# Batched attention with an FFN behind it: score halves and column groups in stretches of sixteen products, and a written order of products from step 48

## The chip, the cores and the metric

The kernel runs on one core of one Trainium2 chip. The metric is the device time of one execution in microseconds. Matrix products run on TensorE (PE), and everything they write lands in PSUM, eight banks of 512 f32 columns on 128 partitions. ScalarE (ACT) and VectorE (DVE) empty those banks, GpSimd (POOL) does elementwise work in SBUF, and SyncE (SP) issues nearly all DMAs.

## What is computed

Eight batches of eight heads, 576 tokens, 64 channels. A first attention packs keys and values into 32 slots a head; a second lets the queries read these slots; a leaky FFN of 2048 columns follows, all in f32.

```python
p_packed = sm_attn(p, k, v)                 # 32 packed slots a head
out = sm_attn(q, p_packed, p_packed)        # B, H, S, D
x = transpose(out).reshape(4608, 512)
h = x @ w_in                                # 512 -> 2048
g = maximum(h, 0) + alpha * minimum(h, 0)
return g @ w_out                            # 2048 -> 512
```

## The kernel before

**Halves and steps.** A batch has two halves of 288 tokens, `k = 2b` and `2b + 1`. The FFN of a half goes through 16 blocks `f` of 128 columns, so a batch takes 32 steps and the program 256, each with one `first(k, f)` and one `second(k, f)`. The kernel never forms x: it multiplies the packed values p' by w_in once a batch (`packed_w`, four column groups `j` of 512 columns, each written as a pair of numbers hi and lo that add up to f32), and `first` multiplies these by the attention weights `a` of the second softmax, also held as a pair: six products of 128x128 weights and 288 columns (L572 to L574, three for each half of the heads) into one bank of the pool `ps_h`, which has two. Then ACT takes relu(-h) (`neg`, L580), DVE adds alpha's part (L581), ACT casts that to `gh` (L591), and DVE takes the rest `gl` (L592). Without the flag `from_sbuf` L581 writes its result back into the bank, which is then held until L592 has read it; with it the result goes into `neg` in SBUF, and the bank is free after L581. `second` (L610 to L612) multiplies gh and gl by w_out: twelve products into the four accumulators of `ps_a`, which are copied out after the last block of a half (L627, L629).

**Attention of the next batch** is cut into pieces that run between the steps: `attention(b)` and `packed_w_steps(b)` are generators that do one piece at each step of a list. With T = 32(b - 1) the pieces of batch b lie at steps T + 3 to T + 20, and its four column groups at T + 21, 25, 29 and 33; the first step that needs them is T + 32. Their banks come from `ps_m`, which has two. Scores are taken in halves `hf` of 288 columns: eight products (L317), one for each head, of 64x32 weights, into two banks, one for each `r` of two head groups. Scores of p and k are copied to SBUF by ACT (L360), those of q and p' are transposed into SBUF by DVE (L450). A column group of p' w_in is also eight products of 64x32 weights, with 512 columns (L516), into two banks; ACT (L535) and DVE (L536) both read each bank. The values are packed by forty products of 128x32 weights in one stretch (L428).

**What sets the order.** The program is written in order of steps, `first` of step i, the pieces of step i, `second` of step i - 2, and a scheduler puts the instructions of each engine in an order of its own, by priority and by its estimate of when operands and buffers are ready. `tc.issue_after(ins)` keeps what follows behind an instruction; before, the pieces of a step stand behind `first` of that step (`marks`) by this, but nothing ties one FFN product to another. Two score halves, or two column groups, are therefore two stretches of products with FFN products between them: there are two banks in `ps_m`, and the first pair has to be emptied first.

```python
gs[k, f] = (gh, gl)
...
order += [(k, f, (0, NF)) for k in range(4, 2 * B) for f in range(NF)]
```

## Time and profile before

| | |
|---|---|
| time, median of three runs | 735.76 us (735.74 to 736.73) |
| span of the profiled execution | 733.9 us |
| PE busy | 715.7 us, 98% of the span |
| PE weight loads busy | 648.9 us |
| DVE, ACT, POOL busy | 421.4, 355.7, 59.7 us |
| granted PE clock | full from slice 5 on |
| FFN products (L610 to L612; L572 to L574) | 2976 of 295 to 299 ns; 1440 of 295 to 299 ns |
| column groups of p' w_in with 512 columns (L516) | 480 records of 601 ns |
| scores into ps_m (L317) | 448 records of 415 ns |

The profile states the span of its execution; the time of a run also holds what lies around the span, and the median of the runs is 1.9 us above it. PE products overlap in the array, so a product's duration is longer than the distance to the next one, and the distance is what counts. A product with f32 operands (scores, p' w_in, transposes, packed values) shows as two records, an FFN product as one. A row with x16 is a merged row: its first start, and the time from there to the end of its last record. Rows of the timeline give the start from the beginning of the span, the duration, and in brackets the idle time before and what ended it.

### The profile page before, as it was taken

How to read it: one execution, taken by the hardware profiler on the slowest of the kernel's cores; microseconds unless marked ns; L12 is line 12 of the kernel's file. 1: busy time of each engine (PE TensorE's matmuls, PEld its weight loads, DVE VectorE, ACT ScalarE, POOL GpSimd, SP SyncE). 2: the span in 40 equal slices, each digit the busy share in tenths (PEclk: the TensorE clock that was granted, in tenths of full speed). 3: DMA queues.
4: the chain of work that ended last, by engine and by line, in shares of the span. 5: the costliest groups of instructions: out<-in, count | busy, mean ns of one | idle time of the engine just before them, and what ended most of it. 6: DMA issues, size and time to landing. Idle time of an engine off the chain costs nothing.

```text
span 733.9 us, 15803 instructions
## 1 busy us (share of the span) xinstructions
PE 715.7 (98%) x6346; PEld 648.9 (88%) x6346; DVE 421.4 (57%) x859; ACT 355.7 (48%) x813; POOL 59.7 (8%) x80
## 2 busy tenths in 40 slices
PE   5799999999999999999999999999999999999997
PEld 3466898999889999899989998989988999989997
DVE  3898988857545464545644465453654446453443
ACT  3686698944434343443444543344444434343332
POOL 1001200004000030001200021000300003000000
PEclk8899999999999999999999999999999999999999
DMA  9996554234324222424223241332231401210000
GB/s 301 375 318 223 203 199 147 68 99 155 126 92 146 81 92 108 145 72 130 90 103 104 93 134 63 117 129 92 97 116 66 147 2 38 82 34 1 31 4 34
DMA packets 51386, 85.45 MB, mean 116 GB/s; under 512 B 4464, under 2 KB 31088, under 8 KB 51312
## 3 DMA queue, kind: packets, MB, share of 16 engines
q1 hardware_dynamic: 51024, 84.14, 33.9%
q8 instruction: 50, 0.82, 0.5%
q10 hardware_dynamic: 288, 0.30, 0.1%
q14 instruction: 24, 0.20, 0.1%
HBM read 70.79 MB, written 13.63 MB: 115 GB/s over the span
## 4 chain that ended last, share of the span: by engine, by line
PE 92%; DVE 3%; ACT 2%; DMA 1%; issue 1%; SPq 1%; ACTq 0%; DVEq 0%
PE acc L612 19%; PE acc L610 18%; PE acc L611 18%; PE ps_h L572 9%; PE ps_h L574 9%; PE ps_h L573 9%; PE ps_m L516 4%; PE ps_m L317 2%; PE ps_m L428 1%; DMA vtwo<-in_v 1%; PE ps_h L569 1%; PE ps_m L411 1%; SPq L170 1%; DVE w L134 0%; DVE w L130 0%
## 5 line engine op out<-in xcount | busy, mean ns | idle before, releaser
L610 PE MATMUL acc<-gh,wo 128*128 128x288 f32 x992 | 283.2, 297 | 0.0
L611 PE MATMUL acc<-gh,wo 128*128 128x288 f32 x992 | 282.5, 295 | 0.0
L612 PE MATMUL acc<-gl,wo 128*128 128x288 f32 x992 | 239.6, 299 | 0.0
L581 DVE SCALAR_TENSOR_TENSOR ps_h<-neg,nal,ps_h 128x288 f32<-128x288 f32 x208 | 107.8, 521 | 170.9 <-ACT neg L580 170.3
L580 ACT ACTIVATE neg<-ps_h 128x288 f32<-128x288 f32 x256 | 105.8, 414 | 206.1 <-PE ps_h L574 200.3
L610 PEld LDWEIGHTS acc<-gh,wo 128*128 128x128 f32 x992 | 186.3, 188 | 4.7 <-issue 3.1
L611 PEld LDWEIGHTS acc<-gh,wo 128*128 128x128 f32 x992 | 186.2, 188 | 2.1 <-issue 1.7
L612 PEld LDWEIGHTS acc<-gl,wo 128*128 128x128 f32 x992 | 166.9, 188 | 22.5 <-issue 22.4
L572 PE MATMUL ps_h<-a_h,pw 128*128 128x288 f32 x480 | 143.6, 299 | 0.0
L574 PE MATMUL ps_h<-a_h,pw 128*128 128x288 f32 x480 | 141.9, 296 | 0.0
L573 PE MATMUL ps_h<-a_l,pw 128*128 128x288 f32 x480 | 141.5, 295 | 0.0
L592 DVE TENSOR_TENSOR gl<-ps_h,gh 128x288 fp32r<-128x288 f32 x208 | 94.8, 456 | 77.2 <-ACT gh L591 73.1
L591 ACT CAST gh<-ps_h 128x288 fp32r<-128x288 f32 x208 | 83.1, 399 | 102.3 <-DVE ps_h L581 95.0
L572 PEld LDWEIGHTS ps_h<-a_h,pw 128*128 128x128 f32 x480 | 90.1, 188 | 7.9 <-issue 3.3
L574 PEld LDWEIGHTS ps_h<-a_h,pw 128*128 128x128 f32 x480 | 90.1, 188 | 0.0
L573 PEld LDWEIGHTS ps_h<-a_l,pw 128*128 128x128 f32 x480 | 90.1, 188 | 0.0
L536 DVE SCALAR_TENSOR_TENSOR pw<-ps_m,pw 128x512 fp32r<-128x512 f32 x60 | 38.8, 685 | 1.0 <-ACT pw L535 0.2
L516 PE MATMUL ps_m<-w,p 64*32 64x512 f32 (+1 forms) x544 | 35.5, 583 | 0.2 <-DVE w L134 0.2
L295 POOL MEMSET vraw<- 64x128 f32 x28 | 4.5, 198 | 348.1 <-PE ps_m L428 348.1
L535 ACT ACTIVATE pw<-ps_m 128x512 fp32r<-128x512 f32 x60 | 32.8, 605 | 0.0
L464 POOL TENSOR_TENSOR t<-t,m 128x576 f32<-128x576 f32 x14 | 17.1, 1220 | 122.5 <-DVE m L462 122.5
L591 ACT CAST gh<-neg 128x288 fp32r<-128x288 f32 x40 | 17.5, 440 | 11.5 <-DVE neg L581 10.9
(105 smaller groups left out, 543.7 us busy)
## 6 DMA issues: line engine op xcount, KB each, us to landing
w<-w_whole SPq DMA_DIRECT2D x48, 512.0 KB, 4.1
outT<-ot SPq DMA_DIRECT2D x62, 144.0 KB, 3.6
wraw<-in_w_in SPq DMA_DIRECT2D x8, 1024.0 KB, 11.0
wraw<-in_w_out SPq DMA_DIRECT2D x8, 1024.0 KB, 6.7
xraw<-in_kT SPq DMA_DIRECT2D x28, 288.0 KB, 4.2
xraw<-in_qT SPq DMA_DIRECT2D x28, 288.0 KB, 3.8
vraw<-in_v SPq DMA_DIRECT2D x28, 256.0 KB, 3.6
w_whole<-w SPq DMA_DIRECT2D x6, 512.0 KB, 7.3
```

Source lines behind the costliest of these rows:

```text
L516: nc.tensor.matmul(banks[r][cs, to], p2[b][rs, cs], w[rs, :], start=True, stop=True)
L536: nc.vector.scalar_tensor_tensor(out=lo, in0=ps, scalar=times, in1=fv(hi), op0=ALU.mult, op1=ALU.subtract)
L572: nc.tensor.matmul(x, w[:, 0, i], a_h[:, i], start=(i == 0), stop=False)
L573: nc.tensor.matmul(x, w[:, 0, i], a_l[:, i], start=False, stop=False)
L574: mm = nc.tensor.matmul(x, w[:, 1, i], a_h[:, i], start=False, stop=(i == 1))
L580: nc.scalar.activation(out=neg, in_=x, func=AF.Relu, scale=-1.0),
L581: nc.vector.scalar_tensor_tensor(out=g, in0=neg, scalar=nal[:, f : f + 1], in1=x, op0=ALU.mult, op1=ALU.add),
L591: late[:] = [nc.scalar.copy(out=gh, in_=g)]
L592: nc.vector.tensor_tensor(out=gl, in0=g, in1=fv(gh), op=ALU.subtract)
L610: nc.tensor.matmul(ps, wo_t[f][:, 0, os_], gh, start=begin, stop=False)
L611: nc.tensor.matmul(ps, wo_t[f][:, 1, os_], gh, start=False, stop=False)
L612: mm = nc.tensor.matmul(ps, wo_t[f][:, 0, os_], gl, start=False, stop=end)
```

## The change

From batch 2 on the two halves of the scores of p and k (step T + 4), the two halves of the scores of q and p' (T + 13), and the column groups 0 with 1 (T + 24) and 2 with 3 (T + 33) are written as one stretch of sixteen products each, a *joint*. The first eight of a joint write into the two banks of `ps_h`, under the name `ps_j`, the other eight into those of `ps_m`. In the joint's step the program writes `first(i)`, `second(i - 2)`, the joint, and then, at the next step, `second(i - 1)` ahead of `first(i + 1)`; `first(i + 2)` follows at once, before `second(i)`. From step 48 on each `first` and `second` is kept behind the product written last (`last_pe`, `strict`), and from there `from_sbuf` is set for all steps. `in_turn` does the same for each product of a joint. The w_in groups are loaded in pairs, four DMAs at T + 18 and four at T + 26.

```diff
+        pool, name = (ps_h, "ps_j") if tag == "h" else (ps_a, tag)
+        return pool.tile([P, 512], F32, name=name, tag=tag)
...
+    def in_turn(b, out, lhs, rhs):
+
+        with ExitStack() as held:
+            if b >= EARLY:
+                held.enter_context(tc.issue_after(last_pe[0].ins))
+            mm = nc.tensor.matmul(out, lhs, rhs, start=True, stop=True)
+        last_mm[:] = [mm]
+        if b >= EARLY:
+            last_pe[:] = [mm]
+
     def scores(b, st, xs, hf):
...
-            banks = [bank() for _ in range(2)]
+            banks = [bank("h" if b >= EARLY and hf == 0 else None) for _ in range(2)]
...
             anchor(b, None, d)
-            yield
+            if b < EARLY or hf:
+                yield
...
-        get(0)
-        yield
-        for j in range(NJ):
-            if j + 1 < NJ:
-                get(j + 1)
-            packed_w(b, j)
+        for j in range(0, NJ, 2):
+            get(j)
+            get(j + 1)
+            yield
+            packed_w(b, j, tag="h")
+            packed_w(b, j + 1)
             yield
...
-        add(attention(b), range(T + 3, T + 3 + 18))
-        add(packed_w_steps(b), [T + n for n in (18, 21, 25, 29, 33)])
-    AHEAD = 2
+        add(attention(b), [T + 3 + n + 2 * (n > 7) for n in range(17)], (T + 4, T + 13))
+        add(packed_w_steps(b), [T + n for n in (18, 24, 26, 33)], (T + 24, T + 33))
+    AHEAD, STRICT = 2, 48
...
     for i in range(len(order) + AHEAD):
+        strict = i >= STRICT
+        n = i - AHEAD
+        seconds = [] if n < AHEAD else [(*order[n], n < 8 and order[n][1] < 2 * QF)]
+        if i - 1 in joints:
+            behind(last_pe, second, *seconds.pop())
         if i < len(order):
-            first(*order[i][:2], i < 8 and order[i][1] < 2 * QF, i < 48)
+            behind(
+                last_pe if strict else [],
+                first, *order[i][:2], i < 8 and order[i][1] < 2 * QF, i < 48 or strict,
+            )
...
+        for one in seconds:
+            behind(last_pe if strict else [], second, *one)
+        if i in joints:
+            behind(marks + last_pe, step, joints[i])
...
-        if i >= 2 * AHEAD:
-            second(*order[i - AHEAD], i - AHEAD < 8 and order[i - AHEAD][1] < 2 * QF)
```

What this does to the order of instructions, at three places. On PE, round the scores of p and k of batch 4 (`xraw` is k, `praw` p; `acc` rows belong to `second`, `ps_h` rows to `first`), before:

```order
L574 MATMUL ps_h<-a_h,pw 128x288
L317 MATMUL ps_m<-xraw,praw 32x288 x8
L612 MATMUL acc_3913<-gl,wo_808 128x288
L612 MATMUL acc_3914<-gl,wo_808 128x288
L612 MATMUL acc_3915<-gl,wo_808 128x288
L611 MATMUL acc_3916<-gh,wo_808 128x288
L612 MATMUL acc_3916<-gl,wo_808 128x288
L572 MATMUL ps_h<-a_h,pw 128x288
```

and with the change:

```order
L618 MATMUL acc_3901<-gl,wo_808 128x288
L618 MATMUL acc_3902<-gl,wo_808 128x288
L315 MATMUL ps_j<-xraw,praw 32x288 x8
L315 MATMUL ps_m<-xraw,praw 32x288 x8
L616 MATMUL acc_3899<-gh,wo_808 128x288
L617 MATMUL acc_3899<-gh,wo_808 128x288
L618 MATMUL acc_3899<-gl,wo_808 128x288
L616 MATMUL acc_3900<-gh,wo_808 128x288
```

Before, the second eight score products follow 25 FFN products after the first eight; now the two groups of eight are neighbours, between two `second`s. In the whole program PE had 62 stretches of products with 64x32 weights between products of other shapes, and has 38 now, 24 fewer: four in each of the batches 2 to 7. The products are the same ones in number and shape.

On DVE, the same place, from the L587 (L581 before) of the step of the joint on; `neg` and `ps_h` carry the number of their step's tile, before:

```order
L581 SCALAR_TENSOR_TENSOR ps_h_3965<-neg_3972,nal_109,ps_h_3965 128x288
L592 TENSOR_TENSOR gl_3976<-ps_h_3965,gh_3975 128x288
L581 SCALAR_TENSOR_TENSOR ps_h_4017<-neg_4024,nal_109,ps_h_4017 128x288
L592 TENSOR_TENSOR gl_4028<-ps_h_4017,gh_4027 128x288
L384 TENSOR_REDUCE nmx_4047<-s_t_3979 128x1
L385 TENSOR_SCALAR nmx_4047<-nmx_4047 128x1
L581 SCALAR_TENSOR_TENSOR ps_h_4066<-neg_4073,nal_109,ps_h_4066 128x288
L384 TENSOR_REDUCE nmx_4080<-s_t_3980 128x1
```

and with the change:

```order
L587 SCALAR_TENSOR_TENSOR neg_3972<-neg_3972,nal_109,ps_h_3965 128x288
L598 TENSOR_TENSOR gl_3976<-neg_3972,gh_3975 128x288
L587 SCALAR_TENSOR_TENSOR neg_4036<-neg_4036,nal_109,ps_h_4029 128x288
L392 TENSOR_REDUCE nmx_4059<-s_t_3991 128x1
L587 SCALAR_TENSOR_TENSOR neg_4073<-neg_4073,nal_109,ps_h_4066 128x288
L392 TENSOR_REDUCE nmx_4080<-s_t_3992 128x1
L598 TENSOR_TENSOR gl_4040<-neg_4036,gh_4039 128x288
```

The `gl` of the step after the joint (gl_4040, tile 4029) now stands behind both row maxima (L392) and the L587 of the step after that; before, the `gl` of that step (gl_4028) stood ahead of the first maximum.

The third place is ACT at the joint of step 36, the scores of p and k of batch 2, while w_out is still converted (`mag`, `rest` and `wo` are the pieces of the conversion, `s_t` the scores' copies), before:

```order
L580 ACTIVATE neg_1644<-ps_h_1637 128x288
L149 ACTIVATE mag_1651<-wraw7_1138 128x1024
L360 COPY s_t_1662<-ps_m_1664 128x288
L360 COPY s_t_1663<-ps_m_1665 128x288
L207 ACTIVATE wo6_1582<-mag_1574 128x1024
L591 CAST gh_1647<-neg_1644 128x288
L159 ACTIVATE rest_1652<-wraw7_1138,tiny_106 128x1024
L580 ACTIVATE neg_1707<-ps_h_1700 128x288
```

and with the change:

```order
L586 ACTIVATE neg_1644<-ps_h_1637 128x288
L150 ACTIVATE mag_1651<-wraw7_1138 128x1024
L208 ACTIVATE wo6_1582<-mag_1574 128x1024
L597 CAST gh_1647<-neg_1644 128x288
L160 ACTIVATE rest_1652<-wraw7_1138,tiny_106 128x1024
L368 COPY s_t_1674<-ps_j_1676 128x288
L368 COPY s_t_1675<-ps_j_1677 128x288
L368 COPY s_t_1674<-ps_m_1688 128x288
L161 ACTIVATE rest_1652<-wraw7_1138 128x1024
L368 COPY s_t_1675<-ps_m_1689 128x288
L586 ACTIVATE neg_1719<-ps_h_1712 128x288
```

The copies stand behind the pieces `wo6` and `rest` of the conversion now, the last copy and the next step's relu (neg_1719) behind one more piece, the second `rest`.

## Rows read from the trace of the kernel before

**Rows 1.** Windows: length, busy of PE, PEld, DVE, ACT, POOL, granted clock, DMA share, GB/s.

```profile
200.00:300.00 100.00, 100.00 (x900) 92.23 (x899) 52.90 (x114) 42.12 (x105) 8.09 (x10) 1.00 0.33 111
```

**Rows 2.** The chain of waits: start, us, what; the packed value products, batches 3 and 7.

```profile
242.12 1.25 PE ps_m L428 x80
...
590.98 1.25 PE ps_m L428 x80
```

**Rows 3.** Timeline, TensorE, round the second score half of batch 4: start, us.

```profile
316.80 0.29 PE L611 MATMUL acc<-gh,wo 128*128 128x288 f32 x1
317.03 0.72 PE L317 MATMUL ps_m<-xraw,praw 64*32 64x288 f32 x16
317.67 0.40 PE L572 MATMUL ps_h<-a_h,pw 128*128 128x288 f32 x1
317.91 0.29 PE L573 MATMUL ps_h<-a_l,pw 128*128 128x288 f32 x1
...
322.15 0.29 PE L612 MATMUL acc<-gl,wo 128*128 128x288 f32 x1
```

**Rows 4.** Timeline, TensorE, round one column group of p' w_in.

```profile
116.80 0.29 PE L574 MATMUL ps_h<-a_h,pw 128*128 128x288 f32 x1
117.03 1.09 PE L516 MATMUL ps_m<-w,p 64*32 64x512 f32 x16
118.05 0.40 PE L610 MATMUL acc<-gh,wo 128*128 128x288 f32 x1
118.28 0.29 PE L611 MATMUL acc<-gh,wo 128*128 128x288 f32 x1
```

**Rows 5.** Timeline, TensorE, round sixteen products of 256 columns, batch 1.

```profile
76.47 1.09 PE L516 MATMUL ps_m<-w,p 64*32 64x256 f32 x32
```

**Rows 6.** Timeline, three engines: one FFN step from its last first product on.

```profile
302.06 0.30 PE L574 MATMUL ps_h<-a_h,pw 128*128 128x288 f32 x1
302.45 0.41 ACT L580 ACTIVATE neg<-ps_h 128x288 f32<-128x288 f32 x1 [2.06 <-PE ps_h L574]
302.90 0.52 DVE L581 SCALAR_TENSOR_TENSOR ps_h<-neg,nal,ps_h 128x288 f32<-128x288 f32 x1 [2.02 <-ACT neg L580]
303.89 0.46 DVE L592 TENSOR_TENSOR gl<-ps_h,gh 128x288 fp32r<-128x288 f32 x1 [0.47 <-ACT gh L591]
```

**Rows 7.** Timeline, ScalarE and VectorE: the emptying of score banks.

```profile
317.94 0.70 ACT L360 COPY s_t<-ps_m 128x288 f32<-128x288 f32 x2 [1.19 <-PE ps_m L317]
342.10 0.85 DVE L450 STREAM_TRANSPOSE t<-ps_m 128x288 f32<-128x288 f32 x2 [1.41 <-PE ps_m L317]
```

**Rows 8.** Timeline, three engines: a column group's stretch and the emptying of its banks.

```profile
304.41 1.09 PE L516 MATMUL ps_m<-w,p 64*32 64x512 f32 x16
305.87 1.10 ACT L535 ACTIVATE pw<-ps_m 128x512 fp32r<-128x512 f32 x2
307.11 1.28 DVE L536 SCALAR_TENSOR_TENSOR pw<-ps_m,pw 128x512 fp32r<-128x512 f32 x2
```

**Rows 9.** Timeline, VectorE: a row maximum behind a leaky step.

```profile
319.27 0.52 DVE L581 SCALAR_TENSOR_TENSOR ps_h<-neg,nal,ps_h 128x288 f32<-128x288 f32 x1
319.71 0.75 DVE L384 TENSOR_REDUCE nmx<-s_t 128x1 f32<-128x576 f32 x1
320.37 0.14 DVE L389 TENSOR_SCALAR den<-den 128x1 f32<-128x1 f32 x1
```

**Rows 10.** Groups of instructions, forms apart: the cast from PSUM and from SBUF.

```profile
L591 ACT CAST gh<-ps_h 128x288 fp32r<-128x288 f32 x208 | 83.1, 399 | 102.3 <-DVE ps_h L581 95.0 <-PE acc L611 7.1
L591 ACT CAST gh<-neg 128x288 fp32r<-128x288 f32 x40 | 17.5, 440 | 11.5 <-DVE neg L581 10.9 <-PE acc L611 0.5
```

**Rows 11.** The page, part 6: DMA issues, count, KB each, median us to landing.

```profile
w<-w_whole SPq DMA_DIRECT2D x48, 512.0 KB, 4.1
```

**Rows 12.** Timeline, ScalarE, round the scores of batch 2: two pieces of weight conversion.

```profile
136.93 1.20 ACT L149 ACTIVATE mag<-wraw 128x1024 f32<-128x1024 f32 x1
...
141.29 1.45 ACT L160 ACTIVATE rest<-wraw 128x1024 uint16<-128x1024 uint32 x1
```

More of the change, by code (lines that the diff above doesn't have):

```diff
@@ L89, in pack_attention_ffn_kernel @@
     wo_t, wi_t, p2, result, pw, gs, part, acc, two_pw = {}, {}, {}, {}, {}, {}, {}, [], []
-    marks, late = [], []
+    marks, late, last_pe = [], [], []
     def drain(gen):
@@ L313, in scores @@
         else:
-            banks = [bank() for _ in range(2)]
+            banks = [bank("h" if b >= EARLY and hf == 0 else None) for _ in range(2)]
         for pr, r, rs, cs in heads():
-            last_mm[:] = [
-                nc.tensor.matmul(
-                    banks[r][cs, :HS], st[rs, cs], xs[pr][rs, hf * HS : hf * HS + HS],
-                    start=True, stop=True,
-                )
-            ]
+            in_turn(
+                b, banks[r][cs, :HS], st[rs, cs], xs[pr][rs, hf * HS : hf * HS + HS]
+            )
         return [ps[:, :HS] for ps in banks]
@@ L506, in late_a, with packed_w @@
         split_a[hf] = here
-    def packed_w(b, j, parts=(None,)):
-        banks = [bank() for _ in range(2)]
+    def packed_w(b, j, parts=(None,), tag=None):
+        banks = [bank(tag) for _ in range(2)]
         for part_ in parts:
@@ L514, in packed_w @@
                 w = wi_t[j, pr] if part_ is None else w0[part_][:, pr]
-                last_mm[:] = [
-                    nc.tensor.matmul(
-                        banks[r][cs, to], p2[b][rs, cs], w[rs, :], start=True, stop=True
-                    )
-                ]
+                in_turn(b, banks[r][cs, to], p2[b][rs, cs], w[rs, :])
         to = slice(0, 512) if len(parts) == 2 or parts[0] is None else to
@@ L574, in first @@
             mm = nc.tensor.matmul(x, w[:, 1, i], a_h[:, i], start=False, stop=(i == 1))
+        last_pe[:] = [mm]
         neg = gp.tile([P, HS], F32, name="neg", tag="neg", bufs=2)
@@ L612, in second @@
                 mm = nc.tensor.matmul(ps, wo_t[f][:, 0, os_], gl, start=False, stop=end)
+                last_pe[:] = [mm]
             if not end:
@@ L683, in pack_attention_ffn_kernel, with add @@
     order += [(k, f, (0, NF)) for k in range(4, 2 * B) for f in range(NF)]
-    turns, drains = {}, []
-    def add(gen, steps):
+    turns, joints, drains = {}, {}, []
+    def add(gen, steps, apart=()):
         for at_ in steps:
-            turns.setdefault(at_, []).append(gen)
+            (joints if at_ in apart else turns).setdefault(at_, []).append(gen)
         drains.append((steps[-1], gen))
@@ L694, in pack_attention_ffn_kernel, with behind, step @@
         T = 32 * (b - 1)
-        add(attention(b), range(T + 3, T + 3 + 18))
-        add(packed_w_steps(b), [T + n for n in (18, 21, 25, 29, 33)])
-    AHEAD = 2
-    for i in range(len(order) + AHEAD):
+        add(attention(b), [T + 3 + n + 2 * (n > 7) for n in range(17)], (T + 4, T + 13))
+        add(packed_w_steps(b), [T + n for n in (18, 24, 26, 33)], (T + 24, T + 33))
+    AHEAD, STRICT = 2, 48
+    def behind(anchors, what, *args):
+        with ExitStack() as held:
+            for ins in anchors:
+                held.enter_context(tc.issue_after(ins.ins))
+            what(*args)
+    def step(gens):
+        for gen in gens:
+            next(gen, None)
+    for i in range(len(order) + AHEAD):
+        strict = i >= STRICT
[3 more added lines that the diff above has]
+            behind(last_pe, second, *seconds.pop())
         if i < len(order):
-            first(*order[i][:2], i < 8 and order[i][1] < 2 * QF, i < 48)
+            behind(
+                last_pe if strict else [],
+                first, *order[i][:2], i < 8 and order[i][1] < 2 * QF, i < 48 or strict,
+            )
         if i == AHEAD - 1:
-            for n in range(AHEAD):
-                second(*order[n], True)
-        with ExitStack() as behind:
-            for mark in marks:
-                behind.enter_context(tc.issue_after(mark.ins))
-            go(pieces.get(i, ""))
-            for gen in turns.get(i, []):
-                next(gen, None)
+            for m in range(AHEAD):
+                second(*order[m], True)
+        behind(marks, go, pieces.get(i, ""))
+        behind(marks, step, turns.get(i, []))
+        for end, gen in drains:
+            if end == i and i not in joints:
+                behind(marks, drain, gen)
+        for one in seconds:
+            behind(last_pe if strict else [], second, *one)
+        if i in joints:
+            behind(marks + last_pe, step, joints[i])
             for end, gen in drains:
```

1 line of the change is left out of this document (removed).

## The prediction

> **What bounds the kernel now.** I read four views. First the windows: between 200 and 300 us PE is busy 100.00 of 100.00 at a granted clock of 1.00, VectorE half, ScalarE 42% [rows 1]. PE overlaps its products, so that alone does not say they stand close together. The chain of waits does: the forty value products of batch 3 begin at 242.12 and those of batch 7 at 590.98, four batches later, so a batch takes 348.86 / 4 = 87.2 us, all on PE [rows 2]. The timeline of PE says what these 87.2 us are. FFN products follow each other at 0.132 us: from 317.91 to 322.15 stand 32 of them (4.24 / 32) [rows 3]. A batch has 32 steps of 18 products, 576 x 0.132 = 76 us; the other 11 us are products of other shapes and what it costs to go to them and back. So time is to be had only in those 11 us, and any wait that the change brings to PE is paid in full.
>
> What going there and back costs is read in the same view. Round a score half, the last FFN product starts at 316.80 and the second one after the scores at 317.91: 1.11 us, less two ordinary distances of 0.132, is 0.846 for eight products of 288 columns [rows 3]. Round a column group it is 118.28 - 116.80 - 0.264 = 1.216 for eight products of 512 columns [rows 4]. Eight products, one in each of eight tiles of the array, at two lengths: (1.216 - 0.846) / 224 = 1.65 ns a column, so 0.476 of the score half and 0.846 of the column group are work, and 0.37 us of either is fixed. It lies in the start (317.03 - 316.80 - 0.132 = 0.10), in the end (317.91 - 317.67 - 0.132 = 0.11) and in the rest between, the array running empty. That a second round adds its work alone is seen too: sixteen products of 256 columns took 1.09 us, the same as eight of 512 [rows 4, 5].
>
> **The change part by part.** *Removed:* 24 stretches. Sixteen score products should cost 2 x 0.476 + 0.37 = 1.32 instead of 1.69, two column groups 2.06 instead of 2.43. 24 x 0.37 = 8.9 us off. No gain beyond this: PE had no wait left to lose [rows 1, 2].
>
> *Start of a joint.* It takes both banks of ps_h; one still holds the `first` of its own step. From that `first`'s last product (302.06) to relu is 0.39, to L581 0.84, whose 0.52 ends at 1.36, and with the flag the bank is then free [rows 6]. The joint comes after 12 products: 12 x 0.132 + 0.132 + 0.10 = 1.82. 0.46 us to spare; at T + 1 of the next batch (the joint written T + 33), where copies of the accumulators stand on the same queues, about nothing, but there only the second product of the joint needs that bank. Cost 0, at most 0.1 each.
>
> *End of a joint.* The next `first` needs the first ps_h bank again. Behind a score joint twelve products of `second` run ahead of it: from the joint's start 0.64 + 0.48 to the next FFN product, 0.11, 12 x 0.132, together 2.81. The first two banks can be read 0.91 after the start (317.03 to 317.94), ScalarE empties both in 0.70, VectorE in 0.85 [rows 3, 7]: done by 1.8. Cover left, 1.0. Behind column groups the next `first` comes at 1.02 + 0.85 + 0.11 + 1.58 = 3.56. ScalarE starts 1.46 after the start of the stretch and takes 0.55 a bank; VectorE follows with 0.64 a bank, so from 2.1 on, and the two banks are free at 2.8 and 3.4 [rows 8]. The first is needed at 3.56, the second 0.79 later. Cost 0.
>
> *The written order.* From a `first` to its `second` lie 12 + 6 + 12 + 6 products, 4.75 us, and the chain to the end of gl takes 2.29 (302.06 to 303.89 + 0.46) [rows 6]. The cast from SBUF takes 0.440 instead of 0.399 [rows 10]; it is covered. Behind a joint the distance shrinks to 24 products, and at the scores of p and k gl stands behind two row maxima. Worked out from the joint's start: the last product of `first(T + 5)` starts at 2.81 + 0.66 = 3.47, L587 0.84 later at 4.31, the maximum 0.44 later, the next L587 0.66 after that, and so on [rows 6, 9]: 4.75, 5.41, 5.85, gl at 6.51, done at 6.97. The product that reads it is the 33rd from `first(T + 5)` on: 2.81 + 32 x 0.132 = 7.03. Due almost at once. Between 0 and 0.3 for each of five batches; I take 0.1, since the distances are measured ones: 0.5 us.
>
> *The loads* of w_in come in fours; three of the four for the second joint wait for the first joint, nine steps of 2.4 us ahead of their use, against 4.1 us to landing [rows 11]. The later steps of the attention end by T + 21, T + 32 is when they are due. Both 0; on SP only output stores and the queries of step T + 13 stand behind them.
>
> *Batch 2's first joint* falls into the conversion of w_out, whose pieces hold ScalarE for 1.20 and 1.45 us at a time [rows 12]. ScalarE's order there puts two pieces ahead of that joint's copies and a third ahead of the next relu. From 0 (all covered by the 16 products of `second` behind this joint) to one long piece of each kind, 2.65. I take 0.6, nearer to covered, as 16 products are 2.1 us.
>
> *Sum.* The span was 733.9 us and the median 735.76, so 1.9 lie around it and stay. 735.76 - 8.9 + 0.5 + 0.6 = 728.0.
>
> **The rivals.** *A, loads that cannot be hidden.* The second eight of a joint use the tiles that the first eight still work in. If their weights had to wait until those are done, the array would run empty inside the joint as well, and only start and end, 0.21 us, were saved: 24 x 0.21 = 5.0, the time 735.76 - 5.0 + 1.1 = 731.9. Against it stands the stretch with 32 records, no longer than the one with 16 [rows 4, 5]. The Trainium skill, "TensorE: Matmul & The Clock Gate", Part 3, The mechanism, has this rule: weight loads overlap running products only when the row group differs (it names a background weight buffer as another way). By the first half of that rule this rival holds; the trace does not agree, at 1.09 and 1.09 us. 6%.
>
> *B, slower: the emptying becomes the bound.* If the `first` behind a joint of column groups had to wait for all four banks and not for the first, it would wait for VectorE's fourth read: 2.1 + 4 x 0.64 = 4.7 against 3.56, 1.1 us at each of 12 such joints, 13.7, and 728.0 + 13.7 = 741.7. It decides from 0.74 us a joint on, where two stretches' gain is eaten. For it: both engines read each bank, 2.4 us of reading a joint on VectorE alone. Against it: ps_j is ahead of ps_m in both engines' order, and 0.8 us are to spare at the bank that is due first. The Trainium skill, "TensorEngine Tiling (Array Packing)", Performance Considerations, PSUM Bottleneck, says that tiling speeds up TensorE but not the emptying of PSUM, which may become the bottleneck. By that rule this rival would hold; the rows above leave it room for one bank, not for four. 5%.
>
> *C, no change: the written order waits elsewhere.* The scheduler could move products ahead where VectorE was late; now PE stands. 8.9 / 6 = 1.5 us a batch, two maxima of 0.75 [rows 9] ahead of a gl that is due, would eat it all: about 735.8. Against it VectorE is idle half the time [rows 1] and 2.4 us of cover lie in an ordinary step. 5%.
>
> **How the numbers follow.** The forecast, 728.0, gets 84%. Its own bounds: 726.9 with no wait at all, 726.4 if the fixed part is 0.39, as rows read to 0.01 us allow; with 0.3 at five joints and 2.65 in batch 2, 731.0. The range 726.4 to 731.0 leaves out part of A, B and C, some 15%. This kernel's measurement tells 0.2%, 1.5 us, from no change. Forecast and A are faster, 0.90; C gives the same, 0.04, or a little slower; with B slower is 0.06.
>
> **What would show it.** In the trace after: 38 stretches of such products instead of 62; a score joint of 1.1 us and a column joint of 1.9 from first start to the next FFN product; value products 85.7 us apart (87.2 - 4 x 0.37). A shows as joints of 1.3 and 2.05. B shows as L577 waiting for DVE pw L541, C as L616 or L618 waiting for gl or gh away from joints. The forecast is wrong if batches come out above 86.5 us.

## The result, and the profile after

| | before | after |
|---|---|---|
| median of four runs | 735.75 us (735.69 to 736.73) | 729.21 us (728.10 to 730.73) |
| span of the profiled execution | 733.9 us | 727.7 us |
| stretches of products with 64x32 weights | 62 | 38 |
| batch period | 87.2 us | 85.9 us |

The ratio is 0.9915, with a 95% interval from 0.9898 to 0.9931: faster by 6.5 us, or 0.9%. The forecast was 728.0, the range 726.4 to 731.0.

The window that answers to [rows 1] looks the same as before. TensorE was full and is full; what changed is what it is full of. Columns: length, busy of PE, PEld, DVE, ACT, POOL with counts, granted clock, DMA share, GB/s.

```profile
200.00:300.00 100.00, 100.00 (x904) 95.03 (x903) 53.23 (x115) 43.67 (x107) 8.44 (x10) 1.00 0.33 109
```

Four more records in the same 100 us (904 for 900) is all that this view tells. The chain of waits of the kernel after tells more (start, us, what). It answers to [rows 2]:

```profile
217.98 1.02 PE ps_j L315 x16
219.00 0.86 PE ps_m L315 x16
227.19 0.65 PE ps_j L315 x16
227.84 0.48 PE ps_m L315 x16
245.08 1.25 PE ps_m L436 x80
...
588.59 1.25 PE ps_m L436 x80
```

The value products of batches 3 and 7 are now 343.51 us apart, 85.88 a batch, where the forecast said 85.7. A joint shows as two rows that touch: the second begins where the first ends, at 219.00 and at 227.84. The second eight of a column joint take 0.86 and of a score joint 0.48, against 1.02 and 0.65 for the first. So the second eight cost their work alone, as the prediction had it.

The timeline of TensorE round one score joint answers to [rows 3], and round one column joint to [rows 4]:

```profile
312.98 0.72 PE L315 MATMUL ps_j<-xraw,praw 64*32 64x288 f32 x16
313.49 0.69 PE L315 MATMUL ps_m<-xraw,praw 64*32 64x288 f32 x16
314.11 0.40 PE L616 MATMUL acc<-gh,wo 128*128 128x288 f32 x1
...
280.17 1.09 PE L315 MATMUL ps_j<-w,p 64*32 64x512 f32 x16
281.05 1.06 PE L315 MATMUL ps_m<-w,p 64*32 64x512 f32 x16
282.05 0.40 PE L616 MATMUL acc<-gh,wo 128*128 128x288 f32 x1
```

From the first product of a joint to the next FFN product it is 314.11 - 312.98 = 1.13 us and 282.05 - 280.17 = 1.88. The forecast said 1.1 and 1.9. Taking the two ordinary distances off as the prediction did, a score joint costs 1.33 where two score halves cost 2 x 0.843, and a column joint 2.07 where two groups cost 2 x 1.213: 0.36 saved by either, a shade less by the starts in the trace (0.355 on average). 24 joints save 8.5 us.

Not all of the 8.5 arrives. To leave the start-up out, which is the same code and yet puts the last column group of batch 0 (step 33) anywhere from 124.0 to 126.5 us in the fourteen traces of this study, I count from that group's first product to the last product of the kernel, and call it the *long stretch*: 603.5 us before, 598.4 after, 5.1 less. So 3.4 us were lost on the way. 2.7 of them have a place, and all of it lies between 137 and 179 us, while batch 2 is prepared. The first is its first joint. The timeline of TensorE, and of VectorE for the same time:

```profile
137.31 1.27 PE L315 MATMUL ps_j<-xraw,praw 64*32 64x288 f32 x9
138.16 0.43 PE L315 MATMUL ps_m<-xraw,praw 64*32 64x288 f32 x1
138.37 0.45 PE L315 MATMUL ps_j<-xraw,praw 64*32 64x288 f32 x7
...
139.24 0.40 PE L616 MATMUL acc<-gh,wo 128*128 128x288 f32 x1
```

```profile
136.40 1.23 DVE L162 CUSTOM_DVE_ANT_0 mag<-mag,rest 128x2048 uint16<-128x2048 uint16 x1 [0.82 <-ACT rest L161]
137.54 0.51 DVE L587 SCALAR_TENSOR_TENSOR neg<-neg,nal,ps_h 128x288 f32<-128x288 f32 x1
```

Nine of the first sixteen records run, then the others stand until 138.4. They need the second bank of `ps_h`; L587 reads it last, from 137.54 to 138.05. L587 could have begun at 136.6, when ScalarE's relu for it had ended, but stood behind L162, a piece of the conversion of w_out. The joint lasts 1.93 us instead of 1.13: 0.80 lost, at the joint's start.

The second place is step 49. TensorE, and VectorE:

```profile
177.56 0.29 PE L618 MATMUL acc<-gl,wo 128*128 128x288 f32 x1
178.57 0.40 PE L616 MATMUL acc<-gh,wo 128*128 128x288 f32 x1 [0.72 <-DVE ot L630]
```

```profile
175.96 0.77 DVE L497 STREAM_TRANSPOSE s<-t 128x576 f32<-128x576 f32 x1
176.66 0.42 DVE L630 TENSOR_TENSOR ot<-acc,part 128x288 f32<-128x288 f32 x1
177.00 0.49 DVE L587 SCALAR_TENSOR_TENSOR neg<-neg,nal,ps_h 128x288 f32<-128x288 f32 x1
177.41 0.74 DVE L471 TENSOR_REDUCE m<-t 128x18 f32<-128x576 f32 x1
178.07 1.17 DVE L630 TENSOR_TENSOR ot<-acc,part 128x288 f32<-128x288 f32 x3
```

The products of the next half `k` want the four accumulators back; L630 takes their contents out. One goes at 176.66, three only at 178.07, behind softmax operations (L497, L471). Two products start 1.01 us apart instead of 0.13: 0.88 lost. Right round this wait three more distances are long (0.27, 0.21 and 0.24 us instead of 0.13), so that the place costs 1.2 in all. Three short waits between 144 and 147 us (the largest ends at 145.37 on `gh`) cost 0.7, counted in the same way with the product behind them.

The other 0.7 us have no one place. FFN products that follow each other directly stand 132.7 ns apart in the trace after and 132.5 before; over some 3,900 distances that is 0.7 us. What does it I don't know; it is not the joints, for the distance is 132.7 in e1_split below too, where they are taken apart.

### The profile page after: what moved, and what is told of

It reads as the page before. It is cut to its first block, busy times and chain, and to the rows that moved or that the text cites. A ratio compares the mean times of both kernels' runs of the same rounds, so it can differ in the third digit from the quotient of the medians.

```text
span 727.7 us, 15632 instructions
## 1 busy us (share of the span) xinstructions
PE 709.6 (98%) x6346; PEld 652.7 (90%) x6346; DVE 427.1 (59%) x859; ACT 362.6 (50%) x813; POOL 61.1 (8%) x80
## 4 chain that ended last, share of the span: by engine, by line
PE 88%; DVE 5%; ACT 4%; DMA 1%; issue 1%; SPq 1%; ACTq 0%; DVEq 0%
PE acc L616 18%; PE acc L618 17%; PE acc L617 17%; PE ps_h L577 8%; PE ps_h L579 8%; PE ps_h L578 8%; PE ps_m L315 3%; PE ps_j L315 3%; PE ps_m L436 1%; DMA vtwo<-in_v 1%; PE ps_h L574 1%; PE ps_m L419 1%; ACT rest L161 1%; SPq L171 1%; ACT wo L208 1%
## 5 line engine op out<-in xcount | busy, mean ns | idle before, releaser
L616 PE MATMUL acc<-gh,wo 128*128 128x288 f32 x992 | 292.6, 301 | 0.9 <-DVE ot L630 0.7
L617 PE MATMUL acc<-gh,wo 128*128 128x288 f32 x992 | 287.3, 295 | 0.0
L618 PE MATMUL acc<-gl,wo 128*128 128x288 f32 x992 | 266.1, 296 | 0.0
L587 DVE SCALAR_TENSOR_TENSOR neg<-neg,nal,ps_h 128x288 f32<-128x288 f32 x248 | 126.7, 512 | 174.9 <-ACT neg L586 173.8
L586 ACT ACTIVATE neg<-ps_h 128x288 f32<-128x288 f32 x256 | 105.1, 411 | 190.1 <-PE ps_h L579 180.3
L618 PEld LDWEIGHTS acc<-gl,wo 128*128 128x128 f32 x992 | 177.3, 188 | 0.1
L598 DVE TENSOR_TENSOR gl<-neg,gh 128x288 fp32r<-128x288 f32 x248 | 120.0, 487 | 68.2 <-ACT gh L597 65.0
L597 ACT CAST gh<-neg 128x288 fp32r<-128x288 f32 x248 | 106.9, 432 | 105.7 <-DVE neg L587 102.3
L579 PE MATMUL ps_h<-a_h,pw 128*128 128x288 f32 x480 | 141.9, 296 | 0.0
L577 PE MATMUL ps_h<-a_h,pw 128*128 128x288 f32 x480 | 141.6, 295 | 0.0
L577 PEld LDWEIGHTS ps_h<-a_h,pw 128*128 128x128 f32 x480 | 90.2, 188 | 0.1
L579 PEld LDWEIGHTS ps_h<-a_h,pw 128*128 128x128 f32 x480 | 90.1, 188 | 0.0
L541 DVE SCALAR_TENSOR_TENSOR pw<-ps_j,pw 128x512 fp32r<-128x512 f32 x24 | 15.5, 686 | 13.8 <-ACT pw L540 13.8
L541 DVE SCALAR_TENSOR_TENSOR pw<-ps_m,pw 128x512 fp32r<-128x512 f32 x36 | 23.1, 681 | 0.2 <-ACT pw L540 0.2
L499 POOL TENSOR_TENSOR a_l<-s,a_h 128x576 fp32r<-128x576 f32 x14 | 20.2, 1442 | 29.6 <-ACT a_h L498 29.6
L315 PE MATMUL ps_m<-w,p 64*32 64x512 f32 (+1 forms) x352 | 22.2, 566 | 0.2 <-DVE w L135 0.2
```

Source lines behind the costliest of these rows:

```text
L315: mm = nc.tensor.matmul(out, lhs, rhs, start=True, stop=True)
L541: nc.vector.scalar_tensor_tensor(out=lo, in0=ps, scalar=times, in1=fv(hi), op0=ALU.mult, op1=ALU.subtract)
L577: nc.tensor.matmul(x, w[:, 0, i], a_h[:, i], start=(i == 0), stop=False)
L579: mm = nc.tensor.matmul(x, w[:, 1, i], a_h[:, i], start=False, stop=(i == 1))
L586: nc.scalar.activation(out=neg, in_=x, func=AF.Relu, scale=-1.0),
L587: nc.vector.scalar_tensor_tensor(out=g, in0=neg, scalar=nal[:, f : f + 1], in1=x, op0=ALU.mult, op1=ALU.add),
```

## The experiments

| label | edit | median, us | ratio, 95% | period, us |
|---|---|---|---|---|
| e1_split | one FFN group between a joint's halves | 739.14 | 1.0044 [1.0029, 1.0058] | 87.31 |
| e2_free_order | no written order | 728.38 | 0.9893 [0.9867, 0.9920] | 85.87 |
| e3_scores_later | batch 2's scores two steps later | 729.73 | 0.9913 [0.9892, 0.9934] | 85.87 |
| e4_queries_earlier | batch 2's q with p' two steps earlier | 728.19 | 0.9894 [0.9872, 0.9917] | 85.90 |
| e5_conversions_later | two w_out pieces later | 736.28 | 1.0016 [1.0004, 1.0029] | 85.87 |
| e6_hidden_from_psum | no early copy out of PSUM | 752.45 | 1.0248 [1.0225, 1.0271] | 90.13 |
| e7_banks_swapped | joints start in the common banks | 737.95 | 1.0045 [1.0030, 1.0059] | 86.52 |
| e8_free_order_conversions_later | e2 and e5 | 736.37 | 1.0015 [1.0003, 1.0026] | 85.87 |
| e9_conversions_earlier | two w_out pieces earlier | 730.56 | 0.9933 [0.9916, 0.9949] | 85.87 |
| e10_free_order_earlier | e2 and e9 | 730.02 | 0.9930 [0.9916, 0.9945] | 85.87 |
| e11_columns_only | only column groups joined on four banks | 741.11 | 1.0082 [1.0067, 1.0096] | 88.58 |
| e12_scores_only | only score halves joined | 734.80 | 0.9995 [0.9986, 1.0004] | 86.61 |

Ratios are to runs of the kernel before on the same chip; periods are a quarter of the time between the value products of batches 3 and 7. The kernel before has a median of 735.75 us beside the changed kernel, and of 736.28 beside e1 to e4, 735.16 beside e5 to e8 and 735.31 beside e9 to e12. A difference of medians across these groups can be off by about 1 us; a period or a long stretch is read inside one trace.

**e1_split: is it the going there and back that is saved?** Plans, banks and written order stay, but one `second` is written between the two eights of every joint.

```diff
             packed_w(b, j, tag="h")
+            yield
             packed_w(b, j + 1)
```

and the same between the score halves, with the second half of each joint taken up behind that `second`.

> The changed kernel with one twelve-product second written between the two groups of eight of every joint; banks, steps, written order and flags stay, and the stretches are 62 again. Theory (a stretch costs a fixed 0.36 us, and the joining alone is the gain): 24 x 0.36 = 8.6 us more than the changed kernel, span about 736, time about 738, value products 87.3 us apart. Rival (the gain comes from the written order, from the FFN's bank being free earlier, or from the four banks): it stays at 729 to 731.

The trace has 62 stretches again. The two score halves of [rows 3]'s batch, TensorE:

```profile
317.00 0.72 PE L315 MATMUL ps_j<-xraw,praw 64*32 64x288 f32 x16
...
319.43 0.71 PE L315 MATMUL ps_m<-xraw,praw 64*32 64x288 f32 x16
```

A score half costs 0.84 and a column group 1.21 as before, and the period is 87.31 us, 1.43 above the changed kernel and within 0.1 of before. The gain hangs on the joining alone. That the run is 3 us slower than before though its period is the same is batch 2 again: its first score half waits 0.8 as the joint did, TensorE stands for 1.5 us from 144.5 on, and a wait of 1.1 ends at 180.45 on the accumulators' copies.

**e2_free_order: what is the written order worth?**

```diff
-        strict = i >= STRICT
+        strict = False
...
-                first, *order[i][:2], i < 8 and order[i][1] < 2 * QF, i < 48 or strict,
+                first, *order[i][:2], i < 8 and order[i][1] < 2 * QF, True,
```

> The changed kernel with no FFN product kept behind another one from step 48 on; the joints, the banks and the flag that keeps the leaky step in SBUF stay. Theory (the written order is worth nothing by itself, the joints are the gain): 38 stretches still, value products 85.9 us apart, time 728 to 730. Rival (the order is what keeps the scheduler from late operands): PE waits of 0.3 us or more behind the joints, batches of 86.5 us and more, time above 732.

The joints are the same 38 stretches, the gap at 178 us is gone, and the long stretch is 597.3 us, 1.1 less. In batches 3 to 7 the order changes nothing (85.87 for 85.88). In batch 2 it costs the 0.9 of step 49: without it six products of `first` (L577 to L579, from 177.95 on) stand where the changed kernel waits, and L630 is as late as before (three at 178.34). The first joint keeps its 1.9 us.

**e3_scores_later, a miss.**

```diff
+        if b == 2:
+            add(attention(b), [T + 5 + n for n in range(17)], (T + 6, T + 13))
...
```

> The changed kernel with the attention of batch 2 two steps later up to its values, so that its first joint stands at step 38 instead of 36 (the joint of q and p' stays at step 45). Theory (its first joint loses 0.80 us because the relu's partner on VectorE stands behind a 1.23 us piece of the conversion of w_out): that joint costs 1.33 us instead of 2.13, the later wait of 0.88 for the accumulators' copies stays, span 0.8 shorter, 726.9. Rival (the loss moves with the joint, since the order of VectorE is made anew): the joint still costs 1.8 or more, span 727.5 to 728.5.

The joint moves from 137 to 141.6 us and costs more, 2.56 instead of 1.93 from first product to the next FFN product:

```profile
143.05 0.47 PE L315 MATMUL ps_j<-xraw,praw 64*32 64x288 f32 x7 [0.76 <-DVE neg L587]
```

It met the next conversion piece: L162 from 141.34 to 142.57 stands right ahead of L587 at 142.49. So it is the pieces, not the step: the rival held, and the run did not lose less by moving.

**e4_queries_earlier: is the gap at 178 us the softmax?** The same line with `[T + 3 + n for n in range(17)], (T + 4, T + 11)`: batch 2's joint of q and p', and the softmax behind it, two steps earlier.

> The changed kernel with the joint of q and p' of batch 2 at step 43 instead of 45, and its second softmax two steps earlier; all else stays. Theory (the wait of 0.88 us near 178 us comes from that softmax's operations on VectorE standing ahead of the accumulators' copies of step 49, together with the column group of step 47): the wait is gone, the first joint keeps its 0.80, span 0.9 shorter, 726.8. Rival (the copies are late by the column group alone): the wait stays, span 727.7.

The gap at 178 us is gone, so VectorE's operations behind that joint did make it. But the long stretch is 598.2, only 0.1 less: a single column group of step 47 now falls into two pieces, one product alone and seven, at 1.17 and 1.21 instead of 1.22 for all eight. One product alone costs nearly as much as eight, which start within 0.05 us of each other in eight tiles. So 1.2 was paid for the 0.9 and the long distances round it.

**e5_conversions_later: is it L162 that holds the first joint?**

```diff
-    ... 33: "0", 34: "O", 36: "O", 47: "1"}
+    ... 33: "0", 37: "O", 39: "O", 47: "1"}
```

> Edit: the last two w_out conversion pieces go from steps 34 and 36 to steps 37 and 39; all else as in the changed kernel. Theory: batch 2's first joint (137.3 to 139.24 there, 1.93 us where the later score joints have 1.13) is long because VectorE's L587, which frees the second bank of ps_h, stands behind one of these pieces (1.23 us). With the piece gone the joint has 1.13 to 1.25 from its first product to the next FFN product, 0.7 to 0.8 us less, and nothing else of the PE changes: about 728.4 us (ratio 0.990), the wait of 0.9 near 178 us stays. Rival (ScalarE's conversions and emptying, the prediction's own reading): the joint keeps about 1.9, 729.2. Second rival (the loss moves with the conversions): the joint is short, but a wait of 0.5 to 0.8 us appears where the pieces now stand, within 10 us after it.

Both halves of the question got an answer. The joint has 1.131 us, like all others: the 0.80 was L162 ahead of L587. But the loss moved with the pieces, as the second rival had it, and grew far beyond its 0.5 to 0.8: ten microseconds later L162 stands ahead of L587 again, VectorE:

```profile
146.68 1.23 DVE L162 CUSTOM_DVE_ANT_0 mag<-mag,rest 128x2048 uint16<-128x2048 uint16 x1 [0.51 <-ACT rest L161]
147.83 0.51 DVE L587 SCALAR_TENSOR_TENSOR neg<-neg,nal,ps_h 128x288 f32<-128x288 f32 x1
```

TensorE waits 4.9 us in all between 141 and 162 us, 2.2 of them at once, and with that its clock falls. The longest of TensorE's waits in this run (us in total, times, longest), and its windows (columns as above):

```profile
PE ps_h L577 <- DVE neg L587: 3.2, 3, 2.2
```

```profile
147.00:148.00 1.00, 0.00 (x0) 0.00 (x0) 1.00 (x2) 1.00 (x2) 0.00 (x0) 0.58 0.00 0
148.00:149.00 1.00, 0.61 (x2) 0.61 (x3) 1.00 (x3) 1.00 (x4) 0.00 (x0) 0.50 0.00 0
...
153.00:154.00 1.00, 1.00 (x6) 1.00 (x6) 0.00 (x0) 0.11 (x1) 0.00 (x0) 0.51 0.00 0
```

From 147.2 to 154.0 the granted clock is 0.50, the 1.2 GHz level (2.4 GHz at 1.00), though TensorE works again from 148.4 on. Products are 0.24 us apart there instead of 0.13, so that of the 5.6 us of work some 2.5 are lost (5.6 x 0.107 / 0.24). With the waits, 4.9, less the joint's 0.8, that is 6.6; the medians differ by 7.1 and the long stretches by 7.7, so that about 1 us has no place.

**e6_hidden_from_psum: what holds the start of a joint at 0?** The diff's flag `from_sbuf` beyond step 48 is taken back.

```diff
-                first, *order[i][:2], i < 8 and order[i][1] < 2 * QF, i < 48 or strict,
+                first, *order[i][:2], i < 8 and order[i][1] < 2 * QF, i < 48,
```

> Edit: after step 48 VectorE's L598 (gl) reads the FFN's bank in PSUM again, as in the kernel before for these steps, in place of the copy in SBUF that L587 made; joints, banks and written order stay. It measures what the start of a joint costs when the banks are freed later. Theory: the second ps_h bank is then held until gl of the last hidden tile ahead of the joint has ended, some 2.35 us after that tile's first product has ended, where the changed kernel's joint wants it 1.8 us after: a wait of 0.5 to 0.6 us at the start of each of the 22 joints behind step 48, 11 to 13 us in all, about 741 us (ratio 1.007), batch period about 88. Rival (the start of a joint has slack that no row shows, since the w_out products in between cover it): within 1 us of the changed kernel, 729 to 730, period 85.9.

The theory held in kind and fell short by half: the run is 23 us slower than the changed kernel. The start of a joint waits as it said. The joint of [rows 3]'s batch, with what follows, TensorE:

```profile
317.70 0.99 PE L315 MATMUL ps_j<-xraw,praw 64*32 64x288 f32 x9
318.27 0.43 PE L315 MATMUL ps_m<-xraw,praw 64*32 64x288 f32 x1
...
319.35 0.40 PE L616 MATMUL acc<-gh,wo 128*128 128x288 f32 x1
325.22 0.40 PE L577 MATMUL ps_h<-a_h,pw 128*128 128x288 f32 x1 [0.86 <-DVE nmx L393]
```

The joint has 1.65 us instead of 1.13. Score joints lose 0.53 each, column joints 0.51 and 0.78 by turns (and 1.3 once): 13.5 us over the 22 joints, a little more than the 11 to 13 expected. What was not expected stands in the last row: one hidden tile later TensorE waits 1.0 us for its bank, and 0.3 behind the other score joint, 6.7 in all; some 3 us more lie in the product behind each such wait, which comes after 0.24 us instead of 0.13, and in shorter waits behind the column joints. `gl`, which frees the bank now, stands behind the two row maxima L392 on VectorE. Two of the waits of the weight loads, 200 to 640 us (us, times, longest):

```profile
PEld ps_j L315 <- DVE gl L598: 9.2, 19, 1.2
PEld ps_h L577 <- DVE nmx L393: 5.4, 5, 1.1
```

So the copy in SBUF is a part of the change without which joints cost more than they save.

**e7_banks_swapped: how near is the end of a joint to a wait?**

```diff
-            banks = [bank("h" if b >= EARLY and hf == 0 else None) for _ in range(2)]
+            banks = [bank("h" if b >= EARLY and hf == 1 else None) for _ in range(2)]
...
-            packed_w(b, j, tag="h")
-            packed_w(b, j + 1)
+            packed_w(b, j)
+            packed_w(b, j + 1, tag="h")
```

> Edit: the first eight of each joint's products write the FFN's two banks no more, but the two common ones, and the second eight write the FFN's. It measures the end of a joint, where the next hidden tiles want the FFN's banks back. Theory: at a column joint the FFN's banks are then freed only when the second group is emptied: 2.1 us after its start by the modelled latency plus three emptyings of 0.64 on each of two engines, about 4.0 us, where the second hidden tile behind the joint wants its bank about 3.6 us after: a wait of 0.4 to 0.6 us at each of 12 column joints, 5 to 7 us in all, about 735 us (ratio 0.999); the score joints (emptied in 0.7) show none and batch 2's first joint gets shorter, as it no longer starts with the bank that VectorE frees late (-0.5 to -0.8). Rival (the end of a joint has more slack than that sum says): 728.5 to 729.5, period 85.9, column joints at 1.88 with no gap behind.

Behind the column joints a hidden tile now waits for VectorE's last reads, as rival B had it, 0.2 us in one gap and 0.1 at the product behind it; the period grows by 0.64 for two of them, 0.32 each. Behind score joints nothing waits. The weight loads' wait for it, 200 to 640 us:

```profile
PEld ps_h L577 <- DVE pw L541: 2.8, 10, 0.3
```

12 x 0.32 are 3.8 of the 8.7 us that the run is slower. The rest is batch 2. Its first joint is shorter, 1.44, as expected, but the scheduler's order then puts pieces of the conversion ahead of the next tile on both engines, L208 ahead of L586 on ScalarE and L209 ahead of L587 on VectorE, and TensorE stands for 2.6 us at 144.5 and gets the low clock behind it:

```profile
146.00:147.00 1.00, 0.00 (x0) 0.00 (x0) 1.00 (x3) 0.00 (x0) 0.00 (x0) 1.00 0.00 0
147.00:148.00 1.00, 0.87 (x4) 0.87 (x5) 1.00 (x3) 0.43 (x1) 0.00 (x0) 0.61 0.00 0
148.00:149.00 1.00, 1.00 (x6) 1.00 (x6) 1.00 (x3) 0.44 (x1) 0.00 (x0) 0.50 0.00 0
```

**e8_free_order_conversions_later** joins the edits of e2 and e5.

> Edit: the written order is left out (as in the run with a free order) and the last two w_out conversion pieces go to steps 37 and 39; joints and the early copy stay. Theory: both losses of batch 2 go, 0.8 at its first joint and 0.9 near 178 us: from the 125 us mark to the last matmul 596.6 to 596.9 us where the changed kernel has 598.4 and the free order alone 597.3; time 727.2 to 727.9 (ratio 0.988). Rival (the scheduler, given other conversions, places the products elsewhere and loses it again): 728.4 or more, with a joint or a gap above 0.5 us somewhere in batch 2.

A miss for the same reason as e5: the joint is 1.13 and the gap at 178 us gone, but the waits from 141 to 162 us and the low clock are there.

**e9_conversions_earlier and e10_free_order_earlier**: the two pieces at steps 32 and 34, with the written order and without.

```diff
-    ... 33: "0", 34: "O", 36: "O", 47: "1"}
+    ... 32: "O", 33: "0", 34: "O", 47: "1"}
```

> Edit: the last two w_out conversion pieces go from steps 34 and 36 to steps 32 and 34, earlier where the run with steps 37 and 39 had them later; all else as in the changed kernel. In VectorE's order the L587 that frees the second bank of ps_h for batch 2's first joint then stands ahead of a piece's L162 again, and the blocks of w_out are ready sooner, not later. Theory: the joint has 1.13 us (-0.8), no wait over 0.5 us follows within 20 us, the wait of 0.9 near 178 us stays: about 728.4 us (ratio 0.990), and 597.5 us from the 125 us mark to the last matmul where the changed kernel has 598.4. Rival (ScalarE and VectorE are so full from 118 to 148 us that any place of the pieces costs the same): the 0.8 comes back as a wait between 125 and 150 us, 729.2; if that wait is above 2 us the granted clock falls behind it, as in the run with the pieces later, and the time is above 731.

> Edit: the pieces at steps 32 and 34 and the written order left out, joints and the copy in SBUF kept. Theory: the two losses of batch 2 are separate, and both go: 596.5 us from the 125 us mark to the last matmul (changed kernel 598.4, free order alone 597.3), about 727.5 us (ratio 0.9885), period 85.9. Rival (the scheduler, with other due times, puts the accumulators' copies or products elsewhere): 728.4 or more and a gap above 0.5 us in batch 2.

The rival held in e10, and in kind in e9, which is 1.4 us above its 729.2. The joint still has 1.75 us, and new waits come before it. ScalarE in e9, ahead of the joint:

```profile
138.07 1.32 ACT L160 ACTIVATE rest<-wraw,tiny 128x1024 f32<-128x1024 f32 x1
139.23 0.48 ACT L597 CAST gh<-neg 128x288 fp32r<-128x288 f32 x1
139.56 0.47 ACT L586 ACTIVATE neg<-ps_h 128x288 f32<-128x288 f32 x1
```

L162 is out of the way here, but L587 starts only at 140.12, because the relu L586 before it is late on ScalarE, behind a piece (L160) and a cast. The new waits of TensorE are 0.2 to 0.4 us twice for the accumulators' copies (L634), which ScalarE reaches late with a piece between them, and 0.6 for a `gh`. The clock stays at 1.00 with these. The long stretch is 599.8 us in e9 and 598.8 in e10. From 120 to 140 us both engines that empty PSUM are nearly full (in the kernel after ScalarE is busy 9.2 of 10 us from 120 to 130 and 10.0 of 10 from 130 to 140, VectorE 9.3 and 8.7), and each of the three places tried for the pieces pays somewhere.

**e11_columns_only, not the test it was meant to be.** The first scores' two halves have no step between them in the code; in the kernel before the scheduler put FFN products between, here the written order keeps them together. So in this run these scores are a joint too, but in the two common banks alone.

```diff
-            banks = [bank("h" if b >= EARLY and hf == 0 else None) for _ in range(2)]
+            banks = [bank() for _ in range(2)]
...
-            if b < EARLY or hf:
-                yield
+            yield
...
-        add(attention(b), [T + 3 + n + 2 * (n > 7) for n in range(17)], (T + 4, T + 13))
+        add(attention(b), range(T + 3, T + 3 + 18))
```

> Edit: the column groups stay joined in pairs, the score halves are single stretches again in steps of their own as in the kernel before; written order and copy in SBUF stay. 50 stretches become 50 - 0: 62 less 12, that is 50. Theory (a joint saves one fixed cost of 0.35, whichever kind): 12 x 0.35 = 4.2 us less than before in the joints, batch period 87.22 - 0.70 = 86.5, batch 2's 0.8 at its first joint gone, the wait near 178 us kept or not: 731.5 to 732.4 us (ratio 0.994 to 0.9955). Rival (the gain hangs on one kind, or on what the joints do to the order): a period of 85.9 or of 87.2, 729 or 735.7.

Neither price came out; the run is 5.8 us slower than before. The trace has 46 stretches, not 50. TensorE in batch 3:

```profile
223.54 0.71 PE L315 MATMUL ps_m<-xraw,praw 64*32 64x288 f32 x16
225.42 1.01 PE L315 MATMUL ps_m<-xraw,praw 64*32 64x288 f32 x16 [1.17 <-ACT s_t L368]
```

The second eight wait until ScalarE has emptied the first two banks (L368). From first product to the next FFN product it is 2.83 us against 1.13 on four banks: 1.34 more than two single halves cost. A half of q and p' loses another 0.66 waiting for p' itself. The column joints have 1.88 us and save 0.36 each as ever: 86.5 + 1.34 + 0.66 = 88.5, measured 88.58. The run shows what the four banks are for.

**e12_scores_only**: column groups in single steps as before (the generator gives one group a step again), score joints as in the change.

```diff
-        add(packed_w_steps(b), [T + n for n in (18, 24, 26, 33)], (T + 24, T + 33))
+        add(packed_w_steps(b), [T + n for n in (18, 21, 25, 29, 33)])
```

> Edit: the score halves stay joined, the column groups are single stretches again in steps of their own; written order and copy in SBUF stay. Theory: 12 x 0.36 = 4.3 us less than before in the joints, batch period 86.5, batch 2's first joint still 1.9 (+0.8), the wait near 178 us kept or not: 731.5 to 733 us (ratio 0.994 to 0.996). The two savings and the losses of batch 2 add up to the change's 6.5. Rival (not additive): the period is not 86.5 within 0.1, or the sum of the two gains differs from the change's by more than 1.5 us beyond the wait near 178 us.

The joints are as in the change, 1.13 us, and 1.93 in batch 2; the gap at 178 us is there. The period is 86.61, 0.61 less than before where two joints should bring 0.72. The time, 0.5 less than before, is outside what I expected: of 4.3 saved, 0.8 and 1.9 go by 179 us, as in the changed kernel, 0.5 in two short waits at 201 and 223 us, and 0.7 in the distances of FFN products, which are 132.7 ns here too. The long stretch is 603.0 us. So of the change's 5.1 there the score pairs, with what goes wrong in batch 2 beside them, bring 0.5, and the column pairs added to them 4.6, near their own 4.2. Since e11 gave no price for the column pairs alone, that the two simply add up is not shown.

## Why the prediction was nearly right

*24 x 0.37 = 8.9 us removed.* Right; by the starts in the trace 0.355 each, 8.5. Rival A, with joints of 1.3 and 2.05, is refuted by 1.13 and 1.88 at every joint but the one in batch 2. How the loads lie shows in the weight loads of the second eight, round the joint at 312.98:

```profile
313.25 0.40 PEld L315 LDWEIGHTS ps_m<-xraw,praw 64*32 64x32 f32 x16
```

Single starts in that trace: these loads begin from 313.25 to 313.30, together with the second records of the first eight in the same eight tiles, and the next products start in those tiles 0.24 us later, at 313.49, the same distance as from there to their own second records at 313.74. So the loads cost no time. The rule behind the rival, in the Trainium skill, "TensorE: Matmul & The Clock Gate", Part 3, The mechanism, is that weight loads overlap running products only when the row group differs. The trace does not agree: here loads begin with products that work in the same rows. The background weight buffer that this section of the Trainium skill names as another way would fit; no run here shows it.

*Start of a joint, cost 0.* Right at 23 joints, and e6 shows on what it rests: the copy in SBUF. Wrong at batch 2's first joint. The 1.36 us to the end of L581 came from a step without a conversion [rows 6]; with L162 ahead, the bank is free 0.8 too late (e5 takes L162 away and the 0.8 with it).

*Batch 2's first joint, 0.6.* The size was near, 0.8, the step was not: I looked for ScalarE behind the joint, and it was VectorE ahead of it. A view of both engines at [rows 12] would have told; L161 stood ahead of L581 there before the change too, where no product wanted the bank. VectorE before:

```profile
136.86 1.23 DVE L161 CUSTOM_DVE_ANT_0 mag<-mag,rest 128x2048 uint16<-128x2048 uint16 x1 [0.82 <-ACT rest L160]
138.00 0.51 DVE L581 SCALAR_TENSOR_TENSOR neg<-neg,nal,ps_h 128x288 f32<-128x288 f32 x1
```

*The written order, 0.5.* Wrong in place. At the score joints `gl` is no wait. It is done when I had worked it out, in batch 4 at 319.93, 6.95 after the joint's start where the sum had 6.97:

```profile
319.48 0.45 DVE L598 TENSOR_TENSOR gl<-neg,gh 128x288 fp32r<-128x288 f32 x1
```

But the four products that read it come behind eight that read `gh`, the first at 320.82, 0.89 after it; I had it as the third product of that `second`, due at 7.03. The order costs at step 49 instead, 0.88 in one wait and 1.2 in all, where copies of the accumulators stand behind softmax on VectorE. That a fixed order hurts where VectorE is late was rival C's mechanism; I priced it for the joints only, not for the change to the next half `k`. e2 and e4 each take that gap away.

*End of a joint, cost 0.* Right, and rival B's 1.1 us a joint is absent. e7 puts the margin to the test: with the banks swapped I worked out a wait of 0.4 to 0.6, and 0.32 came. The Trainium skill, "TensorEngine Tiling (Array Packing)", Performance Considerations, PSUM Bottleneck, says that the emptying of PSUM may become the bottleneck once tiling has sped TensorE up. The trace agrees in part: no `first` behind a joint of the changed kernel waits for it, and with the other order of banks each column joint does, for 0.32 us.

*The loads, 0.* Right: no product of the long stretch waits for a w_in load.

*Not in the sum:* 0.7 in the short waits from 144 to 147 us and 0.7 in the distances of FFN products, against the change; for it, 0.5 at the start-up and 0.6 behind the last product in the profiled executions. The terms were missed by 0.4 (the stretches), 0.2 (batch 2's first joint), 1.2 (step 49), -0.5 (the written order at the joints) and 1.4 us (these two), 2.7 together, and with -1.1 for the last two that is 1.6. The profiled execution took 729.56 us, 1.6 above the forecast; the median is 1.2 above it. What the joints save was forecast to 0.4 us. That the whole came as near is in part luck: 1.1 us that no term forecast, at the two ends, made up for 2.7 of losses that were too small in the sum, or missing from it.

None of the versions beats the changed kernel beyond doubt. e2 and e4 are 0.8 and 1.0 us below it, with intervals that overlap its own, and ran beside other runs of the kernel before; by the trace e2 gains 1.1 in the long stretch.

## What to carry to other kernels

When TensorE is full, look for what it pays to change the shape of its products, and measure it as first start to next start less the ordinary distance: here 0.36 us each time, and joining two stretches saves just that if every bank they need is free in time. Before joining, follow each bank to the instruction that reads it last, at every stage with other work on that engine, not in a quiet step only. A hand-written order is then worth trying without: it cost nothing in the steady batches and 0.9 us where an engine was late.

## What the runs showed that I had not expected

TensorE's clock falls within a kernel that is 97% busy. After waits of 2.2 us (e5, with three shorter ones just ahead) and of 2.6 us (e7) the granted clock was 0.50, the 1.2 GHz level, for some 6.8 and 3.4 us; one wait of 1.5 us (e1), one of 0.7 (the changed kernel) and several of 0.2 to 0.6 us (e9) left it at 1.00. In e5 the stall of 2.2 us cost 4.7 with the slow products behind it. And the start-up, with the same code, took from 124.0 to 126.5 us, which is more than most of the differences compared here; only spans inside one trace could tell them.
